# A left pad 32 bytes shorter, and block differences of the second mixture made one pair earlier

## The chip, the cores and the metric

The kernel runs on one core of one Trainium2 chip. The metric is the device time of one execution in microseconds. The core's engines work side by side: TensorE (PE) multiplies matrices out of SBUF into PSUM, VectorE (DVE) and ScalarE (ACT) do elementwise work, and SyncE's queue (SP) issues the transfers.

## The reference, cut to what matters

```python
kv = einsum('bhsd,bhse->bhde', k, v)          # attention without softmax
out = einsum('bhsd,bhde->bhse', q, kv)
x = (out / rms(out) * g_norm), heads side by side: [2304, 512]
h = x @ w_in; g = h * clip(h + 3, 0, 6) / 6; x = g @ w_out        # d_ff 2048
p = domain_probs / sum(domain_probs)
for e in range(4):
    out += p[:, e] * (relu(x @ w1[e]) @ w2[e])                    # F = 1024 each
```

Batch 4, 8 heads, 576 positions, head size 64. The result is fp32.

## The kernel before, in words

Three stages follow one another. **Attention** loads q, k and v half a batch at a time and leaves x transposed in SBUF, in five blocks of the 2304 tokens (four of 512 columns and one of 256). **The first feed-forward block** (`ff_in`, lines 340 to 342, and `ff_out`, line 370) takes 16 tiles of its inner width in five units, and in each unit goes over the five token blocks; the sums are kept in SBUF (`acc`). **The second block**, four experts, goes over the tokens in three passes of 768, and in each pass over 16 "quads": an expert and a quarter of its inner width. 48 quads in all.

Products are made to fp32 accuracy from two parts: every operand is split into a high part in the fast fp32 format (fp32r) and the rest, and three matmuls replace one: high x high, high x rest, rest x high. `split` does it with a copy on ACT (line 574) and a subtraction on DVE (line 575).

In a quad the first matrix product is made with Strassen's scheme in Winograd's form: seven half-size products of six 384-column matmuls (`product`, line 687) instead of eight. Its right operands are the seven block sums `xs1` to `xs7` of the tokens, made once a pass by `build`; differences go through the scratch tiles `st1` and `st2` (line 634) and are then split. Its left operands are sums of weight blocks, made for each quad by `convert_in` in the scratch tile `sums` (lines 585 to 590) and split into `win`. The products 1, 6, 2, 5, 7, 3, 4 go by turns into the PSUM banks `qa` and `qb`. After product 2 ACT copies c11 out of PSUM (line 723), after product 3 c12 (line 733); DVE adds c22 (line 729) and c21 (line 736). The relu is split into `g` (ACT line 713, DVE line 716). Then `outs` (line 661) multiplies g with the expert's output weights `wout`, 36 matmuls of 512 columns, each with a 128 x 128 part of g as the loaded weights and wout as the moving operand. In the other lines the moving operands (the ones that stream through PE) are x (340 to 342), gH and gL (370) and xs (687), and the loaded weights are w and win. While outs runs, the next quad's conversions are put into ACT's and DVE's queues a few at a time; when a pass ends, the builds of the next pass go first.

SBUF is filled from both ends. Each tile pool of the left end begins where the last one stopped: constants, then a pad of 48 fp32 numbers, 192 bytes a partition, at byte 4960, and from 5152 on the pools of `acc`, `gH`/`gL`, `r`, x, and later `xs`, `sums`, `st1` and `st2`, all of sizes that are multiples of 512 bytes. 5152 is 10 x 512 + 32, so all these tiles begin 32 bytes past a multiple of 512. The tiles of the right end (`w`, `wout`, `g`, raw weights, at 162816 and up; `win` at 134144 and 148480) begin at multiples of 512.

Only the attention stage has its order written out; elsewhere the order of instructions on each engine is decided when the program is built, by a scheduler that sees which instructions need which tiles. So moving a scratch tile moves instructions.

Of the kernel before, what the change touches and what calls it, by code (L numbers as in the profile page):

```python
# [17 lines left out]
def kernel(  # L18
# [39 lines left out]
    TH = 384  # L58
# [3 lines left out]
    LAG = 3  # L62
    RATE = (4200, 3000, 2600, 2900, 0)
    FMAX = 3.0e38
    PADL, PADR = 48, 248

    const = ctx.enter_context(tc.tile_pool(name="const", bufs=1))
    sp = ctx.enter_context(tc.tile_pool(name="sp", bufs=1))
# [405 lines left out]
    with tc.manual_schedule(engines={mybir.EngineType.PE, mybir.EngineType.Activation, mybir.EngineType.DVE}):  # L474
# [7 lines left out]
        for i in range(NHB + 1):  # L482
# [7 lines left out]
            nxt = i + 1 < NHB  # L490
# [63 lines left out]
    sums = xsp.tile([P, 4, 2, P], F32, tag="sums", name="sums")  # L554
    st1 = xsp.tile([P, 2, TH], F32, tag="st1", name="st1")
    st2 = xsp.tile([P, 2, TH], F32, tag="st2", name="st2")
# [15 lines left out]
    def split(dst, src):  # L572

        nc.scalar.activation(out=dst[0], in_=src, func=AF.Copy)  # L574
        nc.vector.tensor_tensor(out=dst[1], in0=src, in1=dst[0].bitcast(F32), op=ALU.subtract)  # L575

    def convert_in(k):

        r = raw2[k][:, 0].rearrange("p (c i f) -> p i c f", c=KD, i=2)
        win[k] = w = winp.tile([P, 2, 7, 2, P], F32R, tag="win", name="win")  # L580
        a11, a12, a21, a22 = (r[:, i, 2 * c:2 * c + 2, :] for i in range(2) for c in range(2))
        split([w[:, y, 0:2].rearrange("p m c f -> p (m c) f") for y in range(2)], r[:, 0])
        yield
        split([w[:, y, 2] for y in range(2)], a22)
        nc.vector.tensor_tensor(out=sums[:, 0], in0=a21, in1=a22, op=ALU.add)
        yield
        nc.vector.tensor_tensor(out=sums[:, 1], in0=sums[:, 0], in1=a11, op=ALU.subtract)
        nc.vector.tensor_tensor(out=sums[:, 2], in0=a11, in1=a21, op=ALU.subtract)
        yield
        nc.vector.tensor_tensor(out=sums[:, 3], in0=a12, in1=sums[:, 1], op=ALU.subtract)  # L590
        split([w[:, y, 3:5] for y in range(2)], sums[:, 0:2])
        yield
        split([w[:, y, 5:7] for y in range(2)], sums[:, 2:4])
        yield
# [12 lines left out]
    def build(p):  # L607

        t1, t2 = PASSES[p]

        def pieces(h, c):
            return [(acc[b][:, 2 * c:2 * c + 2, o:o + n], slice(z, z + n)) for b, o, n, z in h]

        b11, b12, b21, b22 = pieces(t1, 0), pieces(t2, 0), pieces(t1, 1), pieces(t2, 1)

        def new(m):
            pool = xp if m in XSHOME else xsp
            xs[m] = pool.tile([P, 2, 2, TH], F32R, tag=XSHOME.get(m, f"xs{m}"), name=f"xs{m}")
            return xs[m]

        def plain(m, b):
            x = new(m)
            for s, z in b:
                split([x[:, y, :, z] for y in range(2)], s)

        def summed(m, dst, a, b):

            x = new(m)
            if not isinstance(a, list):
                a = [(a[:, :, z], z) for _, z in b]  # L630
            if not isinstance(b, list):
                b = [(b[:, :, z], z) for _, z in a]
            for (s, z), (s2, _) in zip(a, b):
                nc.vector.tensor_tensor(out=dst[:, :, z], in0=s, in1=s2, op=ALU.subtract)  # L634
            split([x[:, y] for y in range(2)], dst)

        return {
            1: lambda: plain(1, b11),
            5: lambda: summed(5, st1, b12, b11),
            6: lambda: summed(6, st2, b22, st1),  # L640
            2: lambda: plain(2, b21),
            3: lambda: plain(3, b22),
            7: lambda: summed(7, st1, b22, b12),
            4: lambda: summed(4, st1, b21, st2),
        }
# [46 lines left out]
    def pair(k):  # L692
        return (qa, qb) if k % 2 == 0 else (qb, qa)

    def first_product(k):

        x, y = pair(k)
        product(k, x, 1, True)
        return lambda: nc.scalar.activation(out=y, in_=x, func=AF.Copy)

    def quad(k):


        x, y = pair(k)
        g2[k] = g = [
            wp.tile([P, 2, 2, TH], F32R, tag=f"w{(NA + len(ftiles) + 4 + 2 * (k % 2) + f) % NW}", name="g2")
            for f in range(2)]
        us = xp.tile([P, 2, TH], F32, tag="xh4", name="us")
        cs = xp.tile([P, 2, TH], F32, tag="xl4", name="cs")
        u2, u4, c22, c21, c11, c12 = (z[:, y] for z in (us, cs, st1) for y in range(2))  # L710

        def high(f, t, src, func=AF.Relu):
            nc.scalar.activation(out=g[f][:, 0, t], in_=src, func=func)  # L713

        def low(f, t, src):
            nc.vector.scalar_tensor_tensor(  # L716
                out=g[f][:, 1, t], in0=src, scalar=0.0, in1=g[f][:, 0, t].bitcast(F32),
                op0=ALU.max, op1=ALU.subtract)

        product(k, y, 6, False)  # L720
        nc.scalar.activation(out=u2, in_=y, func=AF.Copy)
        product(k, x, 2, False)
        nc.scalar.activation(out=c11, in_=x, func=AF.Copy)  # L723
        high(0, 0, c11)
        low(0, 0, c11)
        product(k, y, 5, False)
        nc.scalar.activation(out=u4, in_=y, func=AF.Copy)  # L727
        product(k, x, 7, True)
        nc.vector.tensor_tensor(out=c22, in0=x, in1=u4, op=ALU.add)  # L729
        high(1, 1, c22)  # L730
        low(1, 1, c22)
        product(k, y, 3, False)
        nc.scalar.activation(out=c12, in_=y, func=AF.Copy)
        high(0, 1, c12)
        product(k, x, 4, False)
        nc.vector.tensor_tensor(out=c21, in0=x, in1=u2, op=ALU.add)
        low(0, 1, c12)
        high(1, 0, c21)
        low(1, 0, c21)
        win.pop(k)  # L740

    def run(g):
        return lambda: next(g, None)


    load2(0)
    load2(1)
    first = build(0)
    ahead = [first[m] for m in (1, 5, 6, 2, 4)] + [run(convert_in(0))] * 5 + [run(convert_in(1))] * 5
    for n in range(N3 + 1, NI):  # L750
        step(n)
        if ahead:
# [13 lines left out]
    builds = []  # L766
    for k in range(NQ):
        last_of_pass = k + 1 < NQ and quads[k + 1][0] != quads[k][0]
        ci, co = convert_in(k + 1) if 0 < k and k + 1 < NQ else iter(()), convert_out(k)
        side = builds + [run(co), run(co)] + [run(ci)] * 5  # L770
        builds = []
        if last_of_pass:
            nxt = build(quads[k + 1][0])
            side.append(nxt[1])
            builds = [nxt[m] for m in (5, 6, 2, 7, 3, 4)]
        seed()
        every = -(-NI2 * 6 // len(side))
        for z, _ in enumerate(filler):
            if z % every == every - 1 and side:
                side.pop(0)()  # L780
        for x in side:
            x()
        quad(k)
        if k + 1 < NQ:
            seed = first_product(k + 1)
        filler = outs(k)
# [32 lines left out]
```

## Time and profile before

| what | value |
|---|---|
| median of 3 runs | 1242.81 us (1242.66 to 1242.96) |
| the profiled execution's own time | 1242.34 us |
| its span, first instruction to last | 1240.6 us |
| PE busy with matmuls | 1218.1 us, 98% of the span |
| DVE, ACT busy | 770.0 us, 62%; 571.8 us, 46% |
| mean granted clock of PE | 0.993 |

The span is what the profile shows of one execution; the execution's own time is 1.7 us longer. Matmuls overlap in PE, so a busy PE is not necessarily PE at its peak: what counts is how far apart matmuls start.

### The profile page before, as it was taken

Reading aid. Unit: us, or ns where it says so; the run is one execution under the profiler, and the core shown is the slowest. Engines: PE = TensorE matmul, PEld = TensorE weight load, DVE = VectorE, ACT = ScalarE, POOL = GpSimd, SP = SyncE. Lnnn points to the kernel's source line nnn. Section 1 sums busy time; section 2 is a strip of 40 time slices with the busy share of each in tenths; the row PEclk is TensorE's granted clock in tenths of the full one; section 3 lists DMA queues with packets and bytes.
Section 4 is the critical chain, followed back from the end, with each engine's and each line's share of the span. In section 5 each row is a group of like instructions: output and inputs, shape, how many; then the busy total and the mean of one; then the engine's idle time right before and its main releaser. Section 6 shows DMA issues by size and latency. Waiting matters only on the chain.

```text
span 1240.6 us, 17493 instructions
## 1 busy us (share of the span) xinstructions
PE 1218.1 (98%) x7068; PEld 1065.6 (86%) x7069; DVE 770.0 (62%) x1469; ACT 571.8 (46%) x1122; POOL 1.6 (0%) x13
## 2 busy tenths in 40 slices
PE   6989999999999999999999999999999999999998
PEld 5868888888888889999999989999999899999997
DVE  5789999673533565565656576656565866565643
ACT  5767454432322334444444454444444644444442
POOL 0000000000000000000000000000000000000000
PEclk9989999999999999999999999999999999999999
DMA  9613222110010001221122122111111221111101
GB/s 342 222 35 100 71 86 68 35 52 1 9 60 1 1 1 68 69 68 68 68 68 69 68 85 101 69 66 67 64 67 66 82 92 67 65 67 68 68 34 51
DMA packets 60832, 87.14 MB, mean 70 GB/s; under 512 B 5200, under 2 KB 37968, under 8 KB 60752
## 3 DMA queue, kind: packets, MB, share of 16 engines
q1 hardware_dynamic: 60752, 86.03, 20.4%
q8 instruction: 55, 0.90, 0.3%
q14 instruction: 25, 0.20, 0.1%
HBM read 81.30 MB, written 4.72 MB: 69 GB/s over the span
## 4 chain that ended last, share of the span: by engine, by line
PE 93%; DVE 4%; ACT 1%; issue 1%; DMA 0%; SPq 0%; DVEq 0%
PE po L661 30%; PE po L370 16%; PE qa L687 14%; PE qb L687 14%; PE ph L340 5%; PE ph L341 5%; PE ph L342 5%; PE po L254 1%; DVE acc L677 1%; DVE xs L575 1%; DVE st L634 1%; PE pq L221 1%; DMA qin<-in_q_dram 0%; PE kvp L236 0%; PE px L311 0%
## 5 line engine op out<-in xcount | busy, mean ns | idle before, releaser
L661 PE MATMUL po<-wout,g 128*128 128x512 f32 x1728 | 400.6, 389 | 0.0
L661 PEld LDWEIGHTS po<-wout,g 128*128 128x128 f32 x1728 | 323.8, 188 | 64.1
L687 PE MATMUL qb<-xs,win 128*128 128x384 f32 x1008 | 205.5, 339 | 1.2 <-ACT us L727 1.2
L687 PE MATMUL qa<-xs,win 128*128 128x384 f32 x1008 | 205.4, 339 | 0.1
L370 PE MATMUL po<-gH,w 128*128 128x512 f32 (+1 forms) x640 | 196.7, 373 | 0.0
L687 PEld LDWEIGHTS qb<-xs,win 128*128 128x128 f32 x1008 | 179.5, 188 | 3.8 <-ACT us L727 1.8
L574 ACT ACTIVATE wout<-raw 128x512 fp32r<-128x512 f32 x96 | 55.4, 624 | 274.9 <-PE po L661 274.9
L687 PEld LDWEIGHTS qa<-xs,win 128*128 128x128 f32 x1008 | 179.7, 188 | 2.7 <-ACT st L723 0.4
L575 DVE TENSOR_TENSOR wout<-raw,wout 128x512 fp32r<-128x512 f32 x96 | 62.2, 688 | 159.2 <-ACT wout L574 159.2
L370 PEld LDWEIGHTS po<-gH,w 128*128 128x128 f32 x640 | 116.8, 188 | 23.4
L348 ACT ACTIVATE r<-ph,three 128x512 f32<-128x512 f32 (+1 forms) x80 | 51.6, 645 | 163.3 <-PE ph L342 163.3
L340 PE MATMUL ph<-xh,w 128*128 128x512 f32 (+1 forms) x320 | 119.7, 374 | 0.0
L370 PE MATMUL po<-gL,w 128*128 128x512 f32 (+1 forms) x320 | 119.2, 373 | 0.0
L342 PE MATMUL ph<-xh,w 128*128 128x512 f32 (+1 forms) x320 | 119.2, 373 | 0.0
L341 PE MATMUL ph<-xl,w 128*128 128x512 f32 (+1 forms) x320 | 119.2, 373 | 0.0
L349 DVE SCALAR_TENSOR_TENSOR r<-r,ph 128x512 f32<-128x512 f32 (+1 forms) x80 | 50.6, 632 | 106.9 <-ACT r L348 106.6
L716 DVE SCALAR_TENSOR_TENSOR g<-st,g 128x384 fp32r<-128x384 f32 x96 | 53.5, 557 | 81.8 <-ACT g L713 81.8
L713 ACT ACTIVATE g<-cs 128x384 fp32r<-128x384 f32 x96 | 49.7, 518 | 60.4 <-DVE cs L729 58.2
L340 PEld LDWEIGHTS ph<-xh,w 128*128 128x128 f32 x320 | 60.2, 188 | 12.6 <-DVE xl L322 0.4
L716 DVE SCALAR_TENSOR_TENSOR g<-cs,g 128x384 fp32r<-128x384 f32 x96 | 53.3, 556 | 28.1 <-ACT g L713 28.1
L341 PEld LDWEIGHTS ph<-xl,w 128*128 128x128 f32 x320 | 60.2, 188 | 11.8
L342 PEld LDWEIGHTS ph<-xh,w 128*128 128x128 f32 x320 | 60.1, 188 | 11.8
(96 smaller groups left out, 1244.3 us busy)
## 6 DMA issues: line engine op xcount, KB each, us to landing
raw<-in_moe_w_dram SPq DMA_DIRECT2D x96, 512.0 KB, 4.2
raw<-in_moe_w_in_dram SPq DMA_DIRECT2D x16, 512.0 KB, 3.6
raw<-in_moe_w_out_dram SPq DMA_DIRECT2D x16, 512.0 KB, 3.6
qin<-in_q_dram SPq DMA_DIRECT2D x8, 576.0 KB, 8.0
kin<-in_k_dram SPq DMA_DIRECT2D x8, 576.0 KB, 6.5
vin<-in_v_dram SPq DMA_DIRECT2D x8, 576.0 KB, 7.3
out_dram<-acc SPq DMA_DIRECT2D x18, 256.0 KB, 2.1
dp<-in_moe_domain_probs_dram SPq DMA_DIRECT2D x1, 36.0 KB, 5.0
```

The lines of the kernel that those rows point to most:

```text
L340: nc.tensor.matmul(ph, lhsT=w[:, 0, c, :], rhs=xH[t][:, c, :], start=(c == 0), stop=False)
L341: nc.tensor.matmul(ph, lhsT=w[:, 0, c, :], rhs=xL[t][:, c, :], start=False, stop=False)
L342: nc.tensor.matmul(ph, lhsT=w[:, 1, c, :], rhs=xH[t][:, c, :], start=False, stop=(c == KD - 1))
L348: lambda: nc.scalar.activation(out=r, in_=ph, func=AF.Relu, bias=three[:, 0:1]),
L349: lambda: nc.vector.scalar_tensor_tensor(out=r, in0=r, scalar=6.0, in1=ph, op0=ALU.min, op1=ALU.mult),
L370: nc.tensor.matmul(po_t[u, t][o], lhsT=lhsT, rhs=rhs, start=(f == 0 and m == 0), stop=(f == UF[u] - 1 and m == 2))
L574: nc.scalar.activation(out=dst[0], in_=src, func=AF.Copy)
L575: nc.vector.tensor_tensor(out=dst[1], in0=src, in1=dst[0].bitcast(F32), op=ALU.subtract)
L661: nc.tensor.matmul(ps[i], lhsT=lhsT, rhs=w[:, f, y], start=(j == 0 and f == 0 and m == 0), stop=(j == FP - 1 and f == 1 and m == 2))
L687: nc.tensor.matmul(bank, lhsT=w[:, wy, AOP[m], c], rhs=xs[m][:, xy, c], start=first and n == 0, stop=n == 5, skip_group_check=True)
L713: nc.scalar.activation(out=g[f][:, 0, t], in_=src, func=func)
L716: nc.vector.scalar_tensor_tensor(out=g[f][:, 1, t], in0=src, scalar=0.0, in1=g[f][:, 0, t].bitcast(F32), op0=ALU.max, op1=ALU.subtract)
```

## The change

The left pad goes from 48 to 40 numbers, from 192 to 160 bytes, and everything behind it moves down by 32 bytes: `acc` begins at 5120, gH at 46080, x at 66560, xs1 at 101376, all multiples of 512. Nothing on the right end moves.

The differences st1 = b12 - b11 and st2 = b22 - st1, which feed block sums 5 and 6, get a step of their own (`diff`, step 0) ahead of the splits (`whole`); for the second and third pass this step is put into the queues while the last quad but one of the pass before runs its outs, and the builds come in the order 6, 5 instead of 5, 6. For that st1 must be free while the last quad runs, so c11 and c12 of every quad go into the first 768 of the 1024 numbers of `sums` instead of st1.

```diff
-    PADL, PADR = 48, 248
+    PADL, PADR = 40, 248
...
-        def summed(m, dst, a, b):
-
-            x = new(m)
+        def diff(dst, a, b):
+
...
             for (s, z), (s2, _) in zip(a, b):
                 nc.vector.tensor_tensor(out=dst[:, :, z], in0=s, in1=s2, op=ALU.subtract)
+
+        def whole(m, dst):
+            x = new(m)
             split([x[:, y] for y in range(2)], dst)
+
+        def summed(m, dst, a, b):
+            diff(dst, a, b)
+            whole(m, dst)
 
         return {
             1: lambda: plain(1, b11),
-            5: lambda: summed(5, st1, b12, b11),
-            6: lambda: summed(6, st2, b22, st1),
+            0: lambda: (diff(st1, b12, b11), diff(st2, b22, st1)),
+            5: lambda: whole(5, st1),
+            6: lambda: whole(6, st2),
...
-        u2, u4, c22, c21, c11, c12 = (z[:, y] for z in (us, cs, st1) for y in range(2))
+        cc = sums.rearrange("p a b c -> p (a b c)")[:, :2 * TH].rearrange("p (y n) -> p y n", y=2)
+        u2, u4, c22, c21, c11, c12 = (z[:, y] for z in (us, cs, cc) for y in range(2))
...
-    ahead = [first[m] for m in (1, 5, 6, 2, 4)] + [run(convert_in(0))] * 5 + [run(convert_in(1))] * 5
+    ahead = [first[m] for m in (1, 0, 5, 6, 2, 4)] + [run(convert_in(0))] * 5 + [run(convert_in(1))] * 5
...
-            side.append(nxt[1])
-            builds = [nxt[m] for m in (5, 6, 2, 7, 3, 4)]
+            side += [nxt[1], nxt[0]]
+            builds = [nxt[m] for m in (6, 5, 2, 7, 3, 4)]
```

The scheduler makes two visible things of it. The counts of instructions stay the same on every engine. First, DVE's queue in a steady quad, from one pair of wout's subtractions to the sums; before:

```order
L575 TENSOR_TENSOR wout<-raw_5687,wout 128x512 x2
L716 SCALAR_TENSOR_TENSOR g_5845<-st_4144,g_5845 128x384
L729 TENSOR_TENSOR cs<-qa,us 128x384
L716 SCALAR_TENSOR_TENSOR g_5846<-cs,g_5846 128x384
L716 SCALAR_TENSOR_TENSOR g_5845<-st_4144,g_5845 128x384
L736 TENSOR_TENSOR cs<-qa,us 128x384
L575 TENSOR_TENSOR win<-raw_5805,win 128x512
L575 TENSOR_TENSOR win<-raw_5805,win 128x256
L716 SCALAR_TENSOR_TENSOR g_5846<-cs,g_5846 128x384
L575 TENSOR_TENSOR win<-sums,win 128x512 x2
L585 TENSOR_TENSOR sums<-raw_5923 128x256
```

and the same place after the change (lines 716, 729, 736 are now 724, 737, 744; cs holds c22 and c21):

```order
L575 TENSOR_TENSOR wout<-raw_5687,wout 128x512 x2
L724 SCALAR_TENSOR_TENSOR g_5845<-sums,g_5845 128x384
L585 TENSOR_TENSOR sums<-raw_5805 128x256
L737 TENSOR_TENSOR cs<-qa,us 128x384
L724 SCALAR_TENSOR_TENSOR g_5846<-cs,g_5846 128x384
L724 SCALAR_TENSOR_TENSOR g_5845<-sums,g_5845 128x384
L744 TENSOR_TENSOR cs<-qa,us 128x384
L575 TENSOR_TENSOR win<-raw_5805,win 128x512
L575 TENSOR_TENSOR win<-raw_5805,win 128x256
L724 SCALAR_TENSOR_TENSOR g_5846<-cs,g_5846 128x384
L587 TENSOR_TENSOR sums<-sums,raw_5805 128x256
L588 TENSOR_TENSOR sums<-raw_5805 128x256
```

Before, the sums of a set of weights were made at the end of the quad ahead of the one in which they are split; now they are made and split in the same quad, and line 585 stands between the first low part and the addition of c22.

Second, DVE's queue where the first pass ends, up to the low part of c11 of the next pass's first quad (acc is the running output, line 677); before:

```order
L634 TENSOR_TENSOR st_4144<-acc_1558,st_4145 128x768
L677 SCALAR_TENSOR_TENSOR acc_5102<-po_6148,prob,acc_5102 128x512
L677 SCALAR_TENSOR_TENSOR acc_5107<-po_6149,prob,acc_5107 128x512
L575 TENSOR_TENSOR xs_6547<-st_4144,xs_6547 128x768
L575 TENSOR_TENSOR win<-sums,win 128x512
L677 SCALAR_TENSOR_TENSOR acc_5115<-po_6150,prob,acc_5115 128x512
L575 TENSOR_TENSOR win<-sums,win 128x512
L716 SCALAR_TENSOR_TENSOR g_6602<-st_4144,g_6602 128x384
```

and after (line 677 is now 684):

```order
L575 TENSOR_TENSOR win<-raw_6403,win 128x256
L585 TENSOR_TENSOR sums<-raw_6403 128x256
L684 SCALAR_TENSOR_TENSOR acc_5102<-po_6148,prob,acc_5102 128x512
L587 TENSOR_TENSOR sums<-sums,raw_6403 128x256
L588 TENSOR_TENSOR sums<-raw_6403 128x256
L684 SCALAR_TENSOR_TENSOR acc_5107<-po_6149,prob,acc_5107 128x512
L590 TENSOR_TENSOR sums<-raw_6403,sums 128x256
L575 TENSOR_TENSOR win<-sums,win 128x512
L684 SCALAR_TENSOR_TENSOR acc_5115<-po_6150,prob,acc_5115 128x512
L575 TENSOR_TENSOR win<-sums,win 128x512
L575 TENSOR_TENSOR wout<-raw_6403,wout 128x512
L724 SCALAR_TENSOR_TENSOR g_6602<-sums,g_6602 128x384
```

The last difference and the last block sum stand further ahead now, and the sums of the weights, which were made a quad earlier before, stand between the accumulations. PE's and ACT's queues move only a few instructions past each other at the same places; SP's queue is the same.

## Rows read from the trace of the kernel before

**Rows 1.** The page, parts 1 and 4: busy time, and the chain that ended last.

```profile
PE 1218.1 (98%) x7068; PEld 1065.6 (86%) x7069; DVE 770.0 (62%) x1469; ACT 571.8 (46%) x1122; POOL 1.6 (0%) x13
...
PE po L661 30%; PE po L370 16%; PE qa L687 14%; PE qb L687 14%; PE ph L340 5%; PE ph L341 5%; PE ph L342 5%; PE po L254 1%; DVE acc L677 1%; DVE xs L575 1%; DVE st L634 1%; PE pq L221 1%; DMA qin<-in_q_dram 0%; PE kvp L236 0%; PE px L311 0%
```

**Rows 2.** Windows: from:to us, length, busy PE, PEld, DVE, ACT, POOL; PEclk, DMA share, GB/s.

```profile
0.00:88.00 88.00, 70.85 (x1434) 57.91 (x1435) 64.44 (x148) 54.53 (x117) 1.65 (x13) 0.93 0.61 211
88.00:487.00 399.00, 398.84 (x1898) 328.98 (x1897) 262.14 (x470) 163.43 (x279) 0.00 (x0) 0.99 0.14 43
...
724.00:745.00 21.00, 20.33 (x102) 17.95 (x102) 19.74 (x30) 13.57 (x26) 0.00 (x0) 1.00 0.34 126
...
978.00:1000.00 22.00, 21.42 (x105) 18.78 (x104) 21.78 (x45) 12.90 (x26) 0.00 (x0) 1.00 0.22 82
...
120.00:200.00 80.00, 80.00 (x369) 65.35 (x368) 76.93 (x140) 39.81 (x67) 0.00 (x0) 1.00 0.26 79
```

**Rows 3.** The chain in order of time: start us, us, engine, line, instructions.

```profile
145.78 2.80 PE po L370 x12
...
284.38 2.80 PE po L370 x12
289.98 2.80 PE po L370 x12
...
477.58 1.40 PE po L370 x12
...
510.10 8.17 PE po L661 x36
```

**Rows 4.** Groups by line and shape: count | busy us, mean ns of one | idle.

```profile
L687 PE MATMUL qb<-xs,win 128*128 128x384 f32 x1008 | 205.5, 339 | 1.2 <-ACT us L727 1.2
...
L370 PE MATMUL po<-gH,w 128*128 128x512 f32 x512 | 172.0, 396 | 0.0
...
L370 PE MATMUL po<-gH,w 128*128 128x256 f32 x128 | 24.7, 279 | 0.0
```

**Rows 5.** Timeline of a steady quad: start us, us, engine, instruction, idle before.

```profile
832.31 1.22 PE L687 MATMUL qa<-xs,win 128*128 128x384 f32 x6
...
835.76 0.56 DVE L729 TENSOR_TENSOR cs<-qa,us 128x384 f32<-128x384 f32 x1 [0.55 <-PE qa L687]
...
836.55 1.22 PE L687 MATMUL qa<-xs,win 128*128 128x384 f32 x6
...
838.67 8.34 PE L661 MATMUL po<-wout,g 128*128 128x512 f32 x36
```

**Rows 6.** Timeline of the first quad of the second block, PE.

```profile
487.04 1.20 PE L687 MATMUL qb<-xs,win 128*128 128x384 f32 x6
...
491.19 1.21 PE L687 MATMUL qb<-xs,win 128*128 128x384 f32 x6
```

**Rows 7.** Groups on DVE by line and shape: count | busy us, mean ns | idle.

```profile
L575 DVE TENSOR_TENSOR wout<-raw,wout 128x512 fp32r<-128x512 f32 x96 | 62.2, 688 | 159.2 <-ACT wout L574 159.2
...
L352 DVE TENSOR_TENSOR gL<-r,gH 128x512 fp32r<-128x512 f32 x64 | 44.0, 687 | 14.2 <-ACT gH L351 13.9
...
L585 DVE TENSOR_TENSOR sums<-raw 128x256 f32<-128x256 f32 x48 | 20.1, 418 | 1.9 <-DMA raw<-in_moe_w_dram 1.9
```

**Rows 8.** Timeline where the first pass ends.

```profile
735.28 1.40 DVE L677 SCALAR_TENSOR_TENSOR acc<-po,prob,acc 128x512 f32<-128x512 f32 x2
...
740.31 0.94 DVE L575 TENSOR_TENSOR xs<-st,xs 128x768 fp32r<-128x768 f32 x1
...
740.43 1.31 PE L687 MATMUL qb<-xs,win 128*128 128x384 f32 x6 [0.58 <-ACT us L727]
...
741.18 0.68 DVE L575 TENSOR_TENSOR win<-sums,win 128x512 fp32r<-128x512 f32 x1
...
741.29 0.49 ACT L723 ACTIVATE st<-qa 128x384 f32<-128x384 f32 x1 [0.91 <-DVE xs L575]
```

**Rows 9.** The page, part 6: loads of the second block's weights, median us to landing.

```profile
raw<-in_moe_w_dram SPq DMA_DIRECT2D x96, 512.0 KB, 4.2
```

## The prediction

> **What bounds the kernel now.** I first read the busy shares and the chain of work that ended last. The matmul engine (PE) is busy 98% of the span, and the chain runs almost wholly through its matmuls: line 661, lines 687, line 370, lines 340 to 342 [rows 1]. The windows by stage say where that holds. Up to 88 us (attention) PE is busy only 70.85 of 88 us; from 88 us to the end of the first feed-forward block at 487 us it is busy 398.84 of 399 us, with the clock granted at 0.99 to 1.00 of its upper level, 2.4 GHz; in the second block it idles only in the two stretches where one pass over the tokens gives way to the next, 0.67 us of 724 to 745 us and 0.58 us of 978 to 1000 us [rows 2]. So from 88 us on the time is the number of matmuls times the distance from one start to the next. A mean duration of a matmul does not give that distance, because matmuls overlap; the pieces of the chain do, since each piece is a run of back-to-back matmuls.
>
> Those pieces show two rates for one shape. Twelve matmuls of line 370 with 512 columns take 2.80 us, 233.3 ns each; thirty-six of line 661, also 512 columns, take 8.17 us, 226.9 ns each [rows 3]. Both load 128 x 128 fp32 weights, use their operands in the same pattern of three, write banks out of the same six, and run at granted clock 1.00. One operand differs: the moving operand of line 370 (gH, gL) begins 32 bytes past a multiple of 512, that of line 661 (wout) at a multiple of 512. Every weight operand of the three lines (w, win, g2) begins at a multiple of 512 already. Lines 340 to 342 read x, which is also 32 bytes off, and run at the slower rate too: the pieces at 284.38 and 289.98 us begin 5.60 us apart, one step of 24 matmuls, twelve of them lines 340 to 342 [rows 3]. VectorE's load does not explain the gap: the 2.80 us stand at 145.78 us, where DVE is busy 76.93 of 80 us, and equally at 289.98 us, in a block in which it is busy 262 of 399 us [rows 2, 3].
>
> **The change, part by part.** *The shorter pad.* After it x, gH, gL and xs begin at multiples of 512, so all moving operands of the two blocks are where wout is now.
>
> 512 columns: line 370 has 512 + 256 of them and lines 340 to 342 have 256 each, 1536 in five groups, one of which stands in [rows 4]. 36 of these lie inside attention, where PE waits anyway, which leaves 1500. The distance falls from 233.3 to 226.9 ns: 1500 x 6.4 = 9.6 us.
>
> 256 columns (the fifth token block): 128 + 64 + 3 x 64 = 384, one group again in [rows 4]. Twelve take 1.40 us, 116.7 ns each [rows 3], half of 233.3, so the loss goes with the columns. I take half of 226.9, 113.5: 384 x 3.2 = 1.2 us.
>
> 384 columns: line 687 has 1008 into each of its two banks [rows 4]. In a steady quad the product that starts at 832.31 us and the outs that start at 838.67 us are 36 matmuls apart: 6.36 us, 176.7 ns each [rows 5]. No aligned 384-column row exists. By columns it would be 226.9 x 384/512 = 170.2: 6.5 ns x 2016 = 13.1 us. The lower end is 0; the nearest row to a middle value is the first quad of the second block, whose four products between 487.04 and 491.19 us take 4.15 us, 172.9 ns each, from the same addresses [rows 6]. That row says that something beside the address moves this rate by 3.8 ns, and the gain could be as small as that or nothing. The upper end for every form is one column per cycle at the granted 2.4 GHz (213.3, 160 and 106.7 ns), 67 us in all, but wout, already at a multiple of 512, does not reach it. I take 13.1 us, because the 256- and 512-column rows agree on a loss per column.
>
> Here a rule stands against the change. The Trainium skill, "SBUF — State Buffer", section "Specifications (TRN2)", says that the memory's lines have 16 bytes, that two hits on a line give the full rate and that crossing to a new line is what costs. A start 32 bytes past a multiple of 512 is on a 16-byte line boundary before and after, so by that rule the pad is worth nothing; the rows of 233.3 and 226.9 ns [rows 3] speak for something coarser than 16 bytes. By the rule the sum would be that of rival 2.
>
> DVE and ACT: no gain or loss. DVE's subtraction takes 688 ns with all operands at multiples of 512 (wout) and 687 ns with all 32 bytes off (gL) [rows 7].
>
> *c11 and c12 move from st1 to the first three quarters of sums.* The scheduler now makes all of a quad's sums within it (the first place shown above). One of them, line 585 at 418 ns [rows 7], stands between the first low part and the addition of c22 (line 729). DVE waits 0.55 us for PE just there, until 835.76 us [rows 5], so 0.42 us fit. The addition must end before the product that starts at 836.55 us writes the same bank; it ends at 836.32, so it could be 0.23 us late before PE waits. Queued behind line 585 are that addition and, through it, ACT's c22. The new wait of c11's copy on the splits of sums costs nothing inside a pass: the splits now end right after a quad, more than 8 us of line 661 before the next c11. Cost 0; if that cover went, 48 quads would each pay what exceeds 0.23 us.
>
> *The differences ahead, pass changes.* At the first change ACT's copy of c11 waits 0.91 us for the split of st1 and starts at 741.29 us, and PE stands 0.58 us for ACT before 740.43 us [rows 8]. st1 no longer stands in the way, and two differences leave DVE's queue there. But c11 must now wait for the first split of sums, which stands late in the same queue (the second place): counted from the accumulations at 735.28 us [rows 8] at the durations of the rows, two accumulations 1.40, a split of xs 0.94, three more accumulations 2.1, five small instructions of 0.42 each [rows 7] and the split 0.68 end at about 742.5 us. What is late next is that split. So the wait is swapped: at best the idle 0.67 + 0.58 = 1.25 us goes, at worst each change loses 1 us more. I take 0. The first build, around 480 us, has PE busy throughout; moved work there I also take at 0.
>
> *DVE in the first block.* From 120 to 200 us DVE is busy 76.93 of 80 us [rows 2]. With PE faster, that stretch takes 80 x 226.9/233.3 = 77.8 us, still more than 76.93; buffers let DVE lag by an item. Cost 0, bound 1 us.
>
> Sum: 9.6 + 1.2 + 13.1 = 23.9 us off the profiled execution's own 1242.34 us (span 1240.6), 1218.4; the median of the runs, 1242.81, is 0.47 above that one, so 1218.9.
>
> **The rivals.** 1. *Only the first block gains, the products little* (0.15). The rate of line 687 follows something else, as the 172.9 ns of the first quad suggest. For it: that row. Against: the same shape of loss per column at 256 and 512. With nothing for the products 1242.81 - 10.8 = 1232.0; with 3.8 ns each, 7.7 us, 1224.3.
>
> 2. *The start address doesn't matter* (0.08): 226.9 against 233.3 ns comes from something else in line 661. For it: no pair of rows differs in the start alone, and the first quad's rate moved with no address. Against: lines 340 and 370 share their rate though their banks, order and partners differ. Then only the pass changes are left, 1242.81 -1.25 to +2, about 1242.8. This is also the case in which the change does not do what its title says.
>
> 3. *Slower* (0.04): line 585 holds up DVE in every quad, because the weights it reads or the low part before it come late, and PE waits for the c22 addition. The price is 48 times what exceeds 0.23 us; it eats the gain and 2.5 us more from 0.23 + (23.9 + 2.5)/48 = 0.78 us late on. Against: the load is asked for a quad earlier (15.6 us: 42 x 176.7 + 36 x 226.9 ns) and takes 4.2 us [rows 9]. At 1 us late: 1218.9 + 37 = 1256.
>
> 4. *More than the sum* (0.04): the products, whose starts after the change fall on 0 and 512 modulo 2048 too, lose less than wout does; at half of wout's loss per column (165 ns) 10 us more, 1209.
>
> **How the numbers follow.** The forecast's own case has 0.69 and, with the pass changes, spans 1216 to 1222. The prediction is its time, 1218.9. Alone it leaves out 0.31, so the range reaches up over rival 1 to 1231 and down to 1213, where it holds about 0.83. A measurement of this kernel can tell about 0.2%, 2.5 us, from no change. Faster: 0.69 + 0.15 + 0.04 = 0.88; the same: 0.08; slower: 0.04.
>
> **What the changed profile would show.** Right: chain pieces of line 370 of 2.72 us for twelve, ends of the first block near 476 us; products at 1.02 us for six; outs still 8.17 us for thirty-six; a quad of 15.3 us for 15.6. DVE's wait before the c22 addition shrinks to about 0.1 us and PE has no new wait inside a pass. At the pass changes ACT's copy of c11 is released by the split of sums, not of st1. Wrong: 2.80 us for twelve of line 370 (rival 2), 1.06 us for six products (rival 1), or a PE wait on DVE in every quad (rival 3). What would make it wrong most easily is the 384-column rate, for which no aligned row exists.

## The result and the profile after

| | before | after |
|---|---|---|
| median of 4 runs | 1242.88 us (1242.66 to 1243.27) | 1230.11 us (1227.71 to 1230.58) |
| profiled execution, span | 1242.34 us, 1240.6 us | 1227.71 us, 1225.9 us |

The ratio is 0.9893, 95% interval 0.9876 to 0.991: faster by 12.8 us, about half of the 23.9 us of the sum. The profiled execution of after is the fastest of its four, so its trace shows a little more than the median does.

The page of after, parts 1 and 4, answers to [rows 1]:

```profile
PE 1203.8 (98%) x7069; PEld 1060.2 (86%) x7069; DVE 774.8 (63%) x1469; ACT 583.9 (48%) x1122; POOL 1.6 (0%) x13
...
PE po L668 32%; PE po L370 16%; PE qa L694 14%; PE qb L694 14%; PE ph L340 5%; PE ph L341 5%; PE ph L342 5%; PE po L254 1%; DVE acc L684 1%; PE pq L221 0%; PE kvp L236 0%; PE px L311 0%; DMA qin<-in_q_dram 0%; DVE xt L276 0%; ACT xh L321 0%
```

PE bounds the kernel as it did. The two DVE pieces of the pass changes (xs L575, st L634) are gone from the chain. The windows of after (columns as in [rows 2]):

```profile
88.00:487.00 399.00, 399.00 (x1948) 339.21 (x1948) 265.40 (x477) 167.51 (x286) 0.00 (x0) 1.00 0.14 43
724.00:745.00 21.00, 20.42 (x106) 18.60 (x105) 16.83 (x36) 11.41 (x23) 0.00 (x0) 1.00 0.33 113
...
120.00:200.00 80.00, 80.00 (x377) 67.16 (x376) 78.03 (x143) 40.67 (x68) 0.00 (x0) 1.00 0.24 77
```

In the same 399 us PE starts 1948 matmuls instead of 1898, at practically the same busy share: each takes less. Which ones, the pieces of the chain of after tell (start us, us, line, instructions), against [rows 3, 5]:

```profile
287.89 2.72 PE po L370 x12
...
463.12 1.44 PE po L370 x12
...
475.85 1.04 PE qb L694 x6
...
483.17 8.20 PE po L668 x36
...
833.95 1.06 PE qa L694 x6
835.01 1.04 PE qb L694 x6
836.05 1.04 PE qa L694 x6
837.09 1.04 PE qb L694 x6
838.13 1.04 PE qa L694 x6
839.18 1.07 PE qb L694 x6
840.25 1.04 PE qa L694 x6
```

Four rates are read here. Twelve matmuls of 512 columns take 2.72 us instead of 2.80, 226.7 ns each: the gain that was forecast. Twelve of 256 columns take 1.44 us instead of 1.40, 120.0 ns instead of 116.7: a loss where a gain was forecast. Six products of 384 columns take 1.04 us instead of 1.06, 173.3 instead of 176.7, not 170.2. And two of the seven products of the quad shown take longer than their neighbours, as do the 36 outs (8.20 instead of 8.17 us). The start times of single matmuls put this down to the first and the sixth product behind the outs (171, 175, 178, 185, 176, 181 and 176, 175, 177, 185, 176, 182 ns from start to start) and to the first nine outs (229, 233, 236, 224, 231, 236, 228, 232, 231). The slow first product and the slow outs are there in every steady quad, the slow sixth product in 25 of the 43 quads whose 42 products run in one piece. PE is busy without a break between 120 and 200 us while DVE is at 78.03 of 80 us: that bound, [rows 2], has not been reached.

The mean times from one start to the next, taken from the start times of every matmul in both traces, give the sum that the change really made. 512 columns: 233.3 to about 227.1 ns, 1500 x 6.2 = 9.3 us. 256 columns: 116.7 to 119.5, 384 x -2.8 = -1.1 us. 384 columns: 176.7 to 174.6 into the one bank and 178.6 to 176.2 into the other, whose mean has the waits of the pass changes in it, 1008 x 2.1 + 1008 x 2.4 = 4.5 us. Outs: 227.1 to 227.8, 1728 x -0.7 = -1.2 us. Together 11.5 us of the 12.8. The rest is within the spread of the runs: the first matmul of the first block starts at 44.13 us in the trace of before, at 42.22 in that of after, and anywhere between 42.10 and 44.84 in the other kernels below, whichever pad they have.

### The profile page after: what moved, and what is told of

It reads as the page before. It is cut to its first block, busy times and chain, and to the rows that moved or that the text cites. A ratio compares the mean times of both kernels' runs of the same rounds, so it can differ in the third digit from the quotient of the medians.

```text
span 1225.9 us, 17537 instructions
## 1 busy us (share of the span) xinstructions
PE 1203.8 (98%) x7069; PEld 1060.2 (86%) x7069; DVE 774.8 (63%) x1469; ACT 583.9 (48%) x1122; POOL 1.6 (0%) x13
## 4 chain that ended last, share of the span: by engine, by line
PE 95%; DVE 2%; ACT 1%; issue 1%; DMA 0%; SPq 0%; DVEq 0%
PE po L668 32%; PE po L370 16%; PE qa L694 14%; PE qb L694 14%; PE ph L340 5%; PE ph L341 5%; PE ph L342 5%; PE po L254 1%; DVE acc L684 1%; PE pq L221 0%; PE kvp L236 0%; PE px L311 0%; DMA qin<-in_q_dram 0%; DVE xt L276 0%; ACT xh L321 0%
## 5 line engine op out<-in xcount | busy, mean ns | idle before, releaser
L370 PE MATMUL po<-gH,w 128*128 128x512 f32 (+1 forms) x640 | 194.2, 369 | 0.0
L575 DVE TENSOR_TENSOR wout<-raw,wout 128x512 fp32r<-128x512 f32 x96 | 62.2, 688 | 171.1 <-ACT wout L574 171.1
L370 PEld LDWEIGHTS po<-gH,w 128*128 128x128 f32 x640 | 117.3, 189 | 20.1
L724 DVE SCALAR_TENSOR_TENSOR g<-sums,g 128x384 fp32r<-128x384 f32 x96 | 53.5, 558 | 81.4 <-ACT g L721 81.4
L574 ACT ACTIVATE win<-sums 128x512 fp32r<-128x512 f32 x96 | 60.7, 632 | 40.2 <-DVE sums L587 37.7
```

The source lines that it names most:

```text
L370: nc.tensor.matmul(po_t[u, t][o], lhsT=lhsT, rhs=rhs, start=(f == 0 and m == 0), stop=(f == UF[u] - 1 and m == 2))
L724: nc.vector.scalar_tensor_tensor(out=g[f][:, 1, t], in0=src, scalar=0.0, in1=g[f][:, 0, t].bitcast(F32), op0=ALU.max, op1=ALU.subtract)
```

## The experiments

**1 and 2: the two halves of the change.** The first kernel is the kernel before with the new pad alone, the second the changed kernel with the old pad:

```diff
-    PADL, PADR = 48, 248
+    PADL, PADR = 40, 248
```

```diff
-    PADL, PADR = 40, 248
+    PADL, PADR = 48, 248
```

> The kernel before with the left pad at 40 elements and nothing else of the change. Theory F (a start at a multiple of 512 bytes costs each matmul a fixed 13 ns beyond its columns, 32 bytes off it costs by columns): all of the gain is here, 512 columns 226.7 ns, 384 columns 173.3, 256 columns 120, time 1228 to 1231 us, the same as the whole change within 1.5 us. Theory O (part of the gain comes from the differences that moved by one pair and from c22 and c12 in other buffers): time 1232 us or more, because the pass changes keep the waits of 0.6 to 0.9 us of before. The prediction's own steps (a loss per column) would have given 1219 and the rows of after already exclude that.

> The changed kernel with the left pad back at 48 elements, so that only the moved differences and the other home of c22 and c12 are left. Theory F: 1242.8 us within 1.5 us, with matmuls of 233.3, 176.7 and 116.7 ns as before. Theory O: 2 us or more below the kernel before (1241 or less). A loss of 1 to 2 us would say that the moves cost something which the pad hid.

Pad alone: 1230.36 us (1229.52 to 1231.6) against 1242.38, ratio 0.9906 (0.9891 to 0.9921). Order alone: 1242.61 us, ratio 1.0001 (0.9993 to 1.001). The gain is the pad's; the moved differences and the other home of c11 and c12 are worth nothing that can be measured (the interval is about 1 us wide either way). Theory O falls.

**3: the matmuls alone.** One moving tile and one weight tile, both at multiples of 2048 bytes; n columns, the moving operand m bytes further on, the weights wo bytes further on:

```
for n, m, wo in configs:
    for i in range(36):
        a = wo // 4 + 128 * (i % 4)
        matmul(t, lhsT=wt[:, a:a + 128], rhs=mov[:, m // 4:m // 4 + n], start=(i == 0), stop=(i == 35))
```

> Leaves the whole computation out: 36 fp32r matmuls in a row for each pair of a width (128 to 512 columns) and a start of the moving operand (bytes past a multiple of 2048), nothing else on the other engines while they run, a different weight slice for each, then the same with weights that start 32 bytes off. The output is not the reference's. Theory F: at a multiple of 512, start to start is 0.4167 ns per column plus 13.3 ns (512: 226.7, 384: 173.3, 256: 120, 128: 66.7); 32 bytes off it is 0.456 ns per column (233.3, 176.7 at most, 116.7, 58.3), so the two cross between 256 and 384 columns. Theory C (the differences between the widths come from the kernel: who else uses SBUF then, or which weights are loaded): alone, all widths at a multiple of 512 follow 0.443 ns per column (512: 226.7, 384: 170, 256: 113.5, 128: 56.7). Theory W (the place of the weights counts too): with weights 32 bytes off the times change by 3 ns or more at an unchanged moving operand. Open: from which start (64, 128 or 256 bytes off) the loss of 6.6 ns at 512 columns is gone.

The timeline of PE (start us, us, instruction; the tile's name gives n, m and wo):

```profile
37.44 4.50 PE L58 MATMUL n256m0w0x<-mov,wt 128*128 128x256 f32 x36
41.78 4.41 PE L58 MATMUL n256m32w0x<-mov,wt 128*128 128x256 f32 x36
46.02 5.43 PE L58 MATMUL n320m0w0x<-mov,wt 128*128 128x320 f32 x36
...
56.57 6.40 PE L58 MATMUL n384m0w0x<-mov,wt 128*128 128x384 f32 x36
62.82 6.40 PE L58 MATMUL n384m32w0x<-mov,wt 128*128 128x384 f32 x36
69.06 7.59 PE L58 MATMUL n448m0w0x<-mov,wt 128*128 128x448 f32 x36
...
83.84 8.34 PE L58 MATMUL n512m0w0x<-mov,wt 128*128 128x512 f32 x36
92.03 8.57 PE L58 MATMUL n512m32w0x<-mov,wt 128*128 128x512 f32 x36
100.43 8.41 PE L58 MATMUL n512m64w0x<-mov,wt 128*128 128x512 f32 x36
...
217.12 8.55 PE L58 MATMUL n512m0w32x<-mov,wt 128*128 128x512 f32 x36
225.51 8.33 PE L58 MATMUL n512m32w32x<-mov,wt 128*128 128x512 f32 x36
233.67 6.41 PE L58 MATMUL n384m0w32x<-mov,wt 128*128 128x384 f32 x36
```

Where no row is left out between two, the difference of their starts is the time of 36 matmuls. The means from one start to the next in ns, without the first four and the last, are

| columns | moving and weights at 0 | moving 32 off | weights 32 off | both 32 off |
|---|---|---|---|---|
| 512 | 226.8 | 233.3 | 233.2 | 226.7 |
| 448 | 206.6 | 204.5 | | |
| 384 | 173.3 | 173.3 | 173.3 | 173.7 |
| 320 | 146.5 | 146.7 | | |
| 256 | 120.0 | 117.7 | 118.4 | 120.0 |
| 192 | 111.7 | 111.7 | | |
| 128 | 111.7 | 111.7 | | |

Three things follow. The rates of after at 512, 384 and 256 columns are those of the matmuls alone, so theory C falls: nothing else in the kernel is needed for them. At equal starts 256, 320, 384 and 512 columns cost 13.2 to 13.5 ns beyond their number divided by the granted 2.4 GHz, a fixed amount and not one by columns, as theory F had it; 448 does not fit (19.9 ns), nor do 128 and 192, which take 111.7 ns at either start where theory F had 66.7 and 58.3 for 128, so this is no law. And what counts at 512 columns is not the start of the moving operand: with the weights 32 bytes off as well it runs at 226.7 ns again, and with them alone off at 233.2. It is the distance between the two starts, which is called the distance from here on. At 512 columns 256, 512 and 1024 bytes are as good as 0 (226.7 to 226.8 ns), 288 and 1056 as bad as 32 (233.3). That was theory W, and it went further than I had thought. One row did not fit: 384 columns run at 173.3 ns at a distance of 32, where the kernel before has 176.7.

**4: the same distance with no left pad touched.** To see whether the distance decides in the kernel too, the right pad, behind which the weights lie, moves them by the 32 bytes by which x, g and block sums are off:

```diff
-    PADL, PADR = 48, 248
+    PADL, PADR = 48, 240
```

> The kernel before with its left pad as it was (48 elements) and the right pad at 240 instead of 248 elements: x, g and block sums still start 32 bytes past a multiple of 512, and now the weights do too, by the same 32 bytes. Theory A (what counts is that the moving operand starts at a multiple of 512 bytes, which is what the change is said to do): nothing moves, 1242.5 us within 1.5 us, and the products of 512 columns with wout as moving operand, which now also starts 32 bytes off, rise from 227 to 233 ns, up to 10 us more. Theory P (what counts is the distance between the starts of the moving operand and of the weights, as the matmuls alone showed: 226.7 ns with both 32 bytes off, 233.2 ns with one of them off): the same gain as with the shorter left pad, 1229 to 1232 us, with 226.7, 173.3 and 120 ns.

1232.39 us (1231.18 to 1232.87) against 1242.37, ratio 0.9922 (0.9907 to 0.9936), just above the 1229 to 1232 of theory P. Its chain:

```profile
450.45 2.72 PE po L370 x12
...
467.14 1.44 PE po L370 x12
...
824.04 1.04 PE qa L687 x6
...
830.31 8.20 PE po L661 x36
```

No moving operand begins at a multiple of 512 here, and the rates are those of after to the last digit; wout, now 32 bytes off together with its weights g2, loses nothing more than in after. Theory A falls: the alignment that the change is named for is not what works, the equal distance is. (The 2 us beyond the left pad's time are not all in these rates; the first block's first matmul starts at 44.84 us here, the latest of all.)

**5: the kernel's own sequences alone.** Quads of seven products and 36 outs on constant data, tiles laid out as in the kernel modulo 2048 bytes; the block sums and win shifted; and twice beside ScalarE copies and VectorE additions:

```
quads("qm0w0", 0, 0); quads("qm32w0", 32, 0); quads("qm32w32", 32, 32); quads("qm64w0", 64, 0)
...
quads("tm0w0", 0, 0)     # beside the other engines
quads("tm32w0", 32, 0)   # beside the other engines
```

> Leaves the whole computation out: the sequences of matmuls of this kernel on constant data, with the starts of before or after, and nothing else on the other engines, except in the last two sequences, where ScalarE copies and VectorE adds 768-element rows all along. Output not the reference's. Sequences q: three quads (products of 384 columns, then the 36 wout matmuls of 512) with block sums 0, 32 or 64 bytes off and win 0 or 32 bytes off; p: products alone; in and ou: the matmuls of lines 340 to 342 and 370 at 512 and 256 columns; t: quads beside the other engines. Theory P: q at distance 0 gives 173.3 ns per product matmul and 226.7 per wout matmul, with both 32 bytes off the same; at distance 32 the products give 176 to 177 ns, because here the planes of x and of the weights alternate as in the kernel, which 36 matmuls on one x slice (173.3 at either start) did not do. Theory E (the loss at 384 columns in the kernel before comes from other engines' traffic): q gives 173.3 at either start and only t shows 176 to 177. For the first product and first outs of a quad (178 and 233 ns in the kernel after): if t alone shows them they come from other engines, if q shows them too they come from the change of width. 256 columns: 120 ns at distance 0, 117 to 119 at every other distance; which is least is open.

The timeline of PE; a trace name drops the digits at its end, so the runs of qm32w up to 129 us are those with the weights at 0, the later ones those with both 32 off:

```profile
51.75 7.47 PE L51 MATMUL qm0w<-xs,win 128*128 128x384 f32 x42
59.05 8.36 PE L51 MATMUL qm0w<-wout,g 128*128 128x512 f32 x36
67.26 7.47 PE L51 MATMUL qm0w<-xs,win 128*128 128x384 f32 x42
...
98.24 7.58 PE L51 MATMUL qm32w<-xs,win 128*128 128x384 f32 x42
105.66 8.34 PE L51 MATMUL qm32w<-wout,g 128*128 128x512 f32 x36
...
145.00 7.45 PE L51 MATMUL qm32w<-xs,win 128*128 128x384 f32 x42
152.29 8.33 PE L51 MATMUL qm32w<-wout,g 128*128 128x512 f32 x36
160.46 7.45 PE L51 MATMUL qm32w<-xs,win 128*128 128x384 f32 x42
...
191.38 7.44 PE L51 MATMUL qm64w<-xs,win 128*128 128x384 f32 x42
198.66 8.34 PE L51 MATMUL qm64w<-wout,g 128*128 128x512 f32 x36
206.84 7.44 PE L51 MATMUL qm64w<-xs,win 128*128 128x384 f32 x42
...
463.60 7.58 PE L51 MATMUL tm32w<-xs,win 128*128 128x384 f32 x42
471.02 8.34 PE L51 MATMUL tm32w<-wout,g 128*128 128x512 f32 x36
```

42 products take 7.30 us (59.05 - 51.75) at distance 0 and 7.42 us (105.66 - 98.24) at 32, by the single starts 174.0 and 176.7 ns each. So the kernel's sequence, in which the planes of x and of the weights alternate, has the loss at 384 columns that 36 matmuls on one slice do not have, and beside busy engines it is the same (471.02 - 463.60 = 7.42 us). Theory E falls; DMA traffic was not tried beside them. The slow first product and first nine outs show in the sequence alone too, almost to the nanosecond (8.21 us, 67.26 - 59.05, for the outs at distance 0, 8.18 at 32 and 64): they come at the change from one sequence to the other, not from another engine. That the change of width makes them is not shown. With block sums and win both 32 bytes off their distance is 0 too and the width changes as often, and yet the outs take 8.17 us (160.46 - 152.29) with the first nine at 226 to 227 ns, and the products 7.29. And in experiment 3 the same stumble, 175, 177, 185, 176 and 182 ns, stands where 384 columns follow 384 columns and only the start of the moving operand moves, to that of the weights. The slow sixth product does not show alone; what starts it in the kernel stays open. At a distance of 64 the first product is as fast as the rest and only the first three outs are slower (229, 233 and 231 ns): 7.28 us for the products, 8.18 for the outs. The matmuls of lines 340 to 342 and 370 at 256 columns took, from start to start, 120.0 ns at distance 0, 117.8 at 32 and 64, 120.0 at 96, 118.6 at 128, 117.3 at 160, 113.4 at 192 and 118.3 at 224; not every other distance is better than 0, as theory P had it, and the one of 192 was not tried in the kernel.

**6 to 9: each term by itself, and a better version.** In the changed kernel the block sums are moved back by 32 bytes (6), moved on by 64 (7), and in (8) the block of 256 columns as well; (9) is the changed kernel once more beside them. The edit of 7 (of 6 with 8 for 16), and what 8 adds (xL and gL are treated as xH and gH):

```diff
+    nc.gpsimd.memset(xsp.tile([P, 16], F32, tag="padx", name="pad"), 0.0)
...
-            xs[m] = pool.tile([P, 2, 2, TH], F32R, tag=XSHOME.get(m, f"xs{m}"), name=f"xs{m}")
+            e = 16 if m in XSHOME else 0
+            x = pool.tile([P, e + 4 * TH], F32R, tag=XSHOME.get(m, f"xs{m}"), name=f"xs{m}")
+            xs[m] = x[:, e:].rearrange("p (y c n) -> p y c n", y=2, c=2)
```

```diff
+    xH = [x[:, (t == 4) * 16:(t == 4) * 16 + KD * n].rearrange("p (c n) -> p c n", c=KD)
+          for x, (t, (_, n)) in zip(xH, enumerate(BLK))]
...
-        gH = gp.tile([P, TB], F32R, tag="gH", name="gH")[:, :n]
+        gH = gp.tile([P, TB], F32R, tag="gH", name="gH")[:, (t == 4) * 16:(t == 4) * 16 + n]
```

> The changed kernel with only the block sums xs moved back to 32 bytes past a multiple of 512; x, g and the weights stay. It measures the term of the products alone. Theory P with the prices of the quads alone (products 176.7 instead of 174.0 ns, wout matmuls 227.0 instead of 227.7, because the slow first product and first outs of a quad come with distance 0): 2016 times 2.7 less 1728 times 0.75, 5.4 less 1.3, 4.1 us above the changed kernel, 1234. The prediction's price (6.5 ns a product) would be 13.1 us above, 1243. If the products' share were nothing (rival 1 of the prediction), 1230.

> The changed kernel with the block sums 64 bytes past a multiple of 512. Theory P with the prices of the quads alone (products 173.4 instead of 174.0 ns, wout 227.0 instead of 227.7, no slow first product and first outs): 2016 times 0.6 and 1728 times 0.75, 2.5 us below the changed kernel, 1227 to 1228.5. Theory A (a multiple of 512 is best for every operand): 2 us or more above it.

> The changed kernel with the block sums 64 bytes off and the moving operands of the block of 256 columns (xh4, xl4 and its gH, gL) 64 bytes off too. Theory P: another 384 times 2.2 ns (120 to 117.8), 0.8 us below the kernel with the sums alone moved, 1226 to 1228 in all. Theory A: above the changed kernel.

> The changed kernel itself once more, so that the three others have it on the same chip: 1230.1 us within 1 us by every theory.

| kernel | median us | ratio to before (95%) |
|---|---|---|
| 6, block sums 32 off | 1232.89 (1232.58 to 1233.56) | 0.9918 (0.9903 to 0.9933) |
| 9, as changed | 1229.64 (1229.0 to 1230.34) | 0.9893 (0.9876 to 0.9909) |
| 7, block sums 64 off | 1227.6 (1227.08 to 1227.76) | 0.9874 (0.9859 to 0.9889) |
| 8, and the short block | 1225.06 (1223.82 to 1227.48) | 0.9857 (0.9842 to 0.9871) |

The chain of kernel 6, then of kernel 7, at the same place:

```profile
822.95 1.06 PE qa L697 x6
...
829.30 8.17 PE po L671 x36
```

```profile
820.04 1.04 PE qb L697 x6
...
827.34 8.17 PE po L671 x36
```

Undoing the products' share of the change costs 3.3 us (1232.89 - 1229.64), a little under the 4.1 expected and a quarter of the 13.1 of the prediction; this is the net of faster products and slower outs. Moving the sums to a distance of 64 gains 2.0 us (2.5 expected), with no slow first product and the outs back at 8.17 us; the fifth and sixth product still stumble in 14 of 43 quads of its trace (185 ns for one or two of their matmuls). Theory A, by which a multiple of 512 is best for every operand, falls once more. Kernel 8 gained 2.5 us more where 0.8 was expected. Its four runs are 3.7 us apart and go with the granted clock, 1223.82 us at 0.996 and 1227.48 at 0.991, so the parts were taken apart below.

**10: other distances, and whose weights.** Two quads for each of eight distances, lines like 370 for eleven, and two sequences in which moving operand and weights both alternate between 0 and 32:

```
w = wf shifted by 32 * (i % 2)
x = gh shifted by 32 * ((i + own) % 2)   # own = 0: the phase of its own weights, own = 1: of the next matmul's
```

> Leaves the whole computation out, matmuls on constant data alone; output not the reference's. First, two quads each with block sums 16, 32, 64, 96, 128, 160, 192 and 224 bytes from the phase of the weights; then 512-column matmuls of the form of line 370 at distances 0, 4, 8, 16, 32, 64, 96, 128, 160, 192 and 224; then two sequences in which both the moving operand and the weights alternate between 0 and 32 bytes: in own, each moving operand has the phase of its own weights and not of the next matmul's; in next, that of the next matmul's weights and not of its own. Theory N (the weights of the next matmul are loaded while this one streams, and what counts is the distance to them): next gives 226.7 ns and own 233. Theory S (the distance to its own weights counts): own 226.7 and next 233. Mixed: both between. For the distances no theory gives numbers beyond 226.7 and 233.3 at 0 and 32 for 512 columns, and 176.7, 173.4 for products at 32 and 64; if the loss falls with distance the products are least from 64 on.

At 512 columns the mean from start to start was 226.7 ns at distance 0, 236.6 at 4, 233.1 at 8, 231.7 at 16, 233.3 at 32, 228.9 at 64, and 233 to 234 from 96 to 224. Products took 173.4 ns at 64, 160 and 224 and 175.5 to 176.7 at 16, 32, 96, 128 and 192. So the loss does not fall with the distance, and no order that I can name lies behind it. In the alternating sequences the moving operand in phase with its own weights took 231.7 ns, in phase with the next matmul's 230.5, in repeating patterns (230, 234, 236 and 227 in the first; 230 nearly throughout in the second). Both means lie between 226.7 and 233, as "mixed" had it; neither N nor S is right, and which load meets which stream stays open.

**11 and 12: the short block alone, and both again.** The edits are the second diff of 6 to 9 alone, and both.

> The changed kernel with only the moving operands of the block of 256 columns 64 bytes off; all else as changed. Theory P: 384 matmuls at 117.8 instead of 119.7 ns, 0.7 us below the changed kernel, 1229 to 1229.5. The prediction's term (256 columns gain 3.2 ns each from a multiple of 512): 1.2 us above it, 1231.3. A gain of 2 us or more, as between the two runs before this one, would say that something beside these 384 matmuls moved.

> The version with the block sums and the block of 256 columns 64 bytes off, once more: theory P 1226.5 to 1227.5 us; its first run gave 1225.1 with a spread of 3.7 us.

1229.55 us (1229.18 to 1230.57), ratio 0.9899 (0.9884 to 0.9914), and 1226.24 us (1225.82 to 1227.44), ratio 0.987 (0.9853 to 0.9886). The chain of kernel 12:

```profile
449.38 2.72 PE po L376 x12
...
466.04 1.41 PE po L376 x12
...
821.87 1.04 PE qb L703 x6
...
827.09 8.17 PE po L677 x36
```

By itself the short block moves the time by less than the runs spread; its rate did change, 1.41 us for twelve instead of 1.44, which is 0.8 us over its 384 matmuls. That speaks against the loss of 1.2 us; the times alone, 0.9899 against 0.9893 with intervals of 0.0015 either way, do not exclude it. Kernel 8's 2.5 us were then mostly spread. Three of the four rates are within 0.01 us a piece of the best that was found (256 columns could go to 113.4 ns). The version is some 3 to 4.5 us below the changed kernel (ratios 0.987 here and 0.9857 in its first run, 0.9893 for the changed kernel), by intervals that lie apart in the first run and overlap in the second.

## Why the prediction was right in part, step by step

The forecast was faster, and it was; 1230.1 us lies in the range of 1213 to 1231, 11 us above the predicted 1218.9. It lies 0.9 us below the range's upper end, in the part that was kept for rival 1; the forecast's own case, 1216 to 1222, did not come true. What came true is nearer to rival 1, "only the first block gains, the products little", whose two prices were 1232.0 and 1224.3 and which had a chance of 0.15.

*What bounds the kernel, and 512 columns.* Right. PE bounds, the two rates of [rows 3] were those of one shape at two distances, and line 370 fell to 226.7 ns: 9.3 of 9.6 us. The reason was put wrongly, though: the prediction noted that all weights begin at multiples of 512 and went on to speak of the moving operand's start. Experiments 3 and 4 show that the distance between the two counts and not the start of the one.

*384 columns, 13.1 us: the step that failed.* "I take 13.1 us, because the 256- and 512-column rows agree on a loss per column." They agreed at a distance of 32 bytes, 116.7 and 233.3 ns, and this was carried over to the new starts, for which only one width had a row. At distance 0 the cost beyond the columns is about the same at 256, 384 and 512 columns: 173.3 ns at 384, 2016 x 3.4 = 6.9 us at most. Of this the slow first product, and in 25 of 43 quads the slow sixth, take some back, and 4.5 us are left in the means, 0.25 of them a wait at the first pass change; the outs lose 1.2 us, which come back where the sums alone are moved (kernels 6 and 7). The products' share of the change, measured by undoing it, is 3.3 us. The 172.9 ns of the first quad [rows 6] had said that a run of products can go at about that rate at the old starts; experiment 3 shows the same, 173.3 ns at a distance of 32 for one slice. In that first quad the rate changes within one run of products, with no start moved, from 172 to 175 ns a matmul to 174 to 180; the timeline of before goes on behind [rows 6] with 1.06 us for six instead of 1.04:

```profile
492.24 1.22 PE L687 MATMUL qa<-xs,win 128*128 128x384 f32 x6
493.30 1.22 PE L687 MATMUL qb<-xs,win 128*128 128x384 f32 x6
```

So the distance alone does not fix the rate at 384 columns; what else does is not shown.

*256 columns, 1.2 us.* The same step, with the wrong sign: 120.0 ns instead of 113.5, a loss of 1.1 us.

*The outs, not costed.* The prediction had them at 8.17 us as before. They became 8.20 with the block sums at their new starts, and are 8.17 again where the sums alone are moved 32 or 64 bytes away from these (kernels 6 and 7).

*DVE in the quad, cost 0.* Right. In the timeline of a steady quad of after, line 585 stands where the order had put it and the addition of c22 follows 0.05 us later (about 0.1 was predicted), so rival 3 does not happen:

```profile
822.25 0.42 DVE L585 TENSOR_TENSOR sums<-raw 128x256 f32<-128x256 f32 x1
...
822.73 0.56 DVE L737 TENSOR_TENSOR cs<-qa,us 128x384 f32<-128x384 f32 x1
```

No distance between matmuls of the second block of after is over 300 ns but one at each pass change.

*The pass changes, cost 0.* Right in size, wrong in what waits. The timeline of after there, against [rows 8]:

```profile
727.96 0.49 ACT L731 ACTIVATE sums<-qa 128x384 f32<-128x384 f32 x1
...
728.11 0.81 PE L694 MATMUL qb<-xs,win 128*128 128x384 f32 x3 [0.58 <-ACT us L735]
```

The copy of c11 no longer waits: the first split of sums was not late as I had worked out. PE's 0.58 us behind ACT's copy of u2 is still there, at both changes, as before. Only a second, short hold-up at the first change (429 ns from start to start in the trace of before, 409 with the pad alone) is gone with the new order, about 0.25 us.

*Rival 2 and the rule beside it.* The pad was given 0.08 to be worth nothing. The Trainium skill, "SBUF — State Buffer", section "Specifications (TRN2)", speaks of 16-byte lines; here distances of 16, 32 and 96 bytes, all whole lines, cost 231.7, 233.3 and 233.6 ns where 0 costs 226.7, so in this case the measurement speaks against reading from it that whole lines are enough.

## What to carry to other kernels

Where two runs of matmuls of one shape show two rates, compare the start of the moving operand with that of its weights, modulo 256 bytes, and time the kernel's own sequence at a few distances before moving anything: the best one differs by width and by sequence (0 at 512 columns, 64 or 224 for these products, 192 at 256). Do not carry a rate from one width to another by columns; a row of the same width at the same starts is worth more than two rows of other widths that agree. A pad is a cheap knob, but it moves everything behind it: price also the operands that were well placed and the neighbours whose rates depend on what runs ahead of them.

## What the runs showed of the hardware that was not expected

- A 32-byte shift of the moving operand costs a 512-column fp32r matmul 6.5 ns (226.8 to 233.3), and the same shift of the weights gives it back (226.7). The 256-column matmul goes the other way: 120.0 at equal starts, 117.7 at 32, 113.4 at 192.
- Where one sequence of matmuls gives way to another, several matmuls can be slower: with products and outs at distance 0, the first product after the outs runs at 171 to 185 ns instead of 173, and the first nine outs at 224 to 236 instead of 227, with no other engine at work. At a distance of 64 for the products only the first three outs are slower, and with block sums and win 32 bytes further on than wout and g none of the first nine is. In the first block of after twelve matmuls of 512 columns take 2.75 us next to steps of 256 columns, and 2.72 otherwise.
- From 192 to 128 columns the time did not fall any more: both took 111.7 ns from start to start, with other weights for each matmul.
- ScalarE copies and VectorE additions beside the quads did not change their rates (42 products in 7.30 us at distance 0 and 7.42 at 32, with and without them).
- Why the distance matters, why it does so without order from 4 to 224 bytes, and why the first products of the second block of before ran at 172.9 ns at the starts at which those of its steady quads took 176.7, was not settled.
